# Windowed attention ahead of two expert layers: deeper buffers and another order for the loads of the attention loop

## The chip, the cores and the metric

The program runs on one core of one Trainium2 chip. The metric is the device time of one launch in microseconds: the median of several runs, lower is better. A profile is one further execution, which the hardware profiler recorded.

## The reference, cut to what matters

Three layers follow each other: attention over short windows, then two mixture-of-experts layers. The change touches the first alone.

```python
B, H, S, D = q.shape                      # 4, 8, 768, 64
chunk, left_ctx, right_ctx = (32, 16, 8)
for c in range(S // chunk):
    q_c = q[:, :, c_start:c_end]
    k_full = np.concatenate([mem_k, k[:, :, l_start:r_end]], axis=2)
    v_full = np.concatenate([mem_v, v[:, :, l_start:r_end]], axis=2)
    scores = scale * np.matmul(q_c, k_full.transpose(0, 1, 3, 2))
    a = np.exp(scores - np.max(scores, axis=-1, keepdims=True))
    a = a / (np.sum(a, axis=-1, keepdims=True) + 1e-09)
    out[:, :, c_start:c_end] = np.matmul(a, v_full)
...
x = attention output as 3072 tokens x 512
x = _moe_ref(x)     # 8 experts, a skip score and a top-1 choice for each token
x = _moe2_ref(x)    # 8 experts, all of them for all tokens, weighted
```

## The kernel before

**The attention loop.** The 3072 tokens are cut into 24 tiles of 128 tokens (`NT`), and the loop `for t in range(NT)` near line 500 is a software pipeline. Step t computes the scores of tile t (`qk`, line 279, on PE), their row maxima (`smax`, DVE) and exponentials (`sexp`, ACT). In the same step PE transposes the exponentials of tile t-1 (`a_trans`), multiplies them with the values (`av`, line 317), and DVE scales the result and starts its store (`x_norm`, lines 323 and 324). Tile t-2 is transposed (`x_trans`), tile t-3 goes through the router's small matmul (`gate1`, `fold`). Every fourth step a group of four tiles gets its routing tables, a chain of small DVE and POOL operations spread over the five steps that follow (`step`); PE's share of it are the rank matmuls (`rank`) in steps 9, 13, 17 and 21 and the table matmuls (`table`) two steps later.

**Loads and stores of a tile.** A tile needs queries (`qs`), windowed keys (`kb`) and windowed values (`vw`). The function `load(i)` starts these three transfers, all but one of them on SyncE's queue (SP in the views), which takes its instructions strictly in program order: an issue that has to wait holds up all issues behind it. `qs` and `kb` have three buffers each and `vw` four. The finished tile goes from `x_nat` (three buffers) to the tensor `x_t` in DRAM. DMA issues on SP count on eight semaphores in turn, so an issue also waits until the transfer eight issues earlier has landed.

**Weights fetched beside the loop.** The first expert layer needs its weights in two parts, a rounded copy and a rest. `fetch()` brings one raw chunk of 512 KB into one of three buffers `wraw` (line 188). `conv` makes the two parts: a copy on ACT (line 192) at once, and two subtractions on DVE (line 196) and the next `fetch()`, which are put on the list `defer` and run in the next step. Steps 4, 7, 11, 15 and 19 convert a chunk (`convs`); three more are converted after the loop (`held`). In the order of a step, the store of tile t-1 comes first, then a fetch if there is one, then the loads of tile t+2:

```python
while defer:
    defer.pop(0)()
if t in (1, 2, 3):
    fetch()
if t + 2 < NT:
    load(t + 2)
if t in convs:
    conv(*first[convs.index(t)], defer)
```

**After the loop** comes the rest of the pipeline for the last tiles, the last routing group of eight tiles, and a gather of the tokens of the first expert (`xe_load`), with which the expert layers begin. PE does matmuls there with little else.

Of the kernel before, what the change touches and what calls it, by code (L numbers as in the profile page):

```python
# [8 lines left out]
F32 = mybir.dt.float32  # L9
# [12 lines left out]
NT = N // 128  # L22
TPB = S // 128
# [3 lines left out]
KWIN = NM + 152 + NM  # L27
KEYS = 96
# [22 lines left out]
def kernel(ctx, tc, qT, kT, v, wg, m1_w1, m1_w2, m2_w1, m2_w2, out):  # L51
    nc = tc.nc
# [3 lines left out]
    def pool(name, **kw):  # L56
        return tc.tile_pool(name=name, bufs=1, reuse_waits="tile", **kw)
# [11 lines left out]
    att = att_s.enter_context(pool("att"))  # L69
# [9 lines left out]
    def bank(name, tag, bufs=1):  # L79
        return psum.tile([128, 512], F32, name=name, tag=tag, bufs=bufs)  # L80


    qs = [att.tile([128, 4, 128], F32, name=f"qs{i}") for i in range(3)]
    kb = [att.tile([128, 4, KWIN], F32, name=f"kb{i}") for i in range(3)]
    vw = [att.tile([KEYS, 2, D], F32, name=f"vw{i}") for i in range(4)]

    def load(i, q=nc.sync):
        b, ib = divmod(i, TPB)
        q.dma_start(out=qs[i % 3], in_=qT[:, b, ib])
        nc.sync.dma_start(out=kb[i % 3], in_=kT[:, b, ib])  # L90
        nc.sync.dma_start(out=vw[i % 4], in_=v[b, ib])


# [1 line left out]
    chunk_bf = att.tile([128, 128], BF16, name="chunk_bf")  # L95
    one = att.tile([128, 1], F32, name="one")

    load(0, nc.scalar)
    nc.gpsimd.memset(chunk_bf, 0.0)
    nc.vector.memset(one, 0.0)  # L100
    nc.scalar.activation(out=one, in_=one, func=ACTF.Exp)
# [1 line left out]
    def fill_mask(i):  # L103
        m = masks[i]
        nc.vector.memset(m, 0.0)
        for j in range(2):
            w = NM * (1 - j)
            nc.vector.memset(m[64 * j:64 * j + 1, :, w + 56:w + WIN], NEG)
            nc.vector.memset(m[64 * j + 32:64 * j + 33, :, w:w + 32], NEG)
        if i == 1:  # L110
            nc.vector.memset(m[0:1, :, NM:NM + 16], NEG)
        if i == 2:
            nc.vector.memset(m[96:97, :, 80:WIN], NEG)
# [4 lines left out]
    fill_mask(0)  # L118
    ident = const.tile([128, 128], F32, name="ident")
    make_identity(nc, ident)  # L120
    load(1)
    ones_bf = keep.tile([128, 128], BF16, name="ones_bf")
    nc.gpsimd.memset(ones_bf, 1.0)
    tri_bf = keep.tile([128, 128], BF16, name="tri_bf")
# [117 lines left out]
    sc = {}  # L242
# [8 lines left out]
    def gate1(i, p=None):  # L251
        p = bank("lp_ps", "A", 3) if p is None else p
        t = xT.pop(i)
        for k in range(KD):
            nc.tensor.matmul(p[32 * k:32 * k + 32, 384:512], wg_sb[:, k], t[:, k], start=True, stop=True, tile_position=(0, 32 * k), skip_group_check=True)
        lp[i] = p

    def lp_evac(i):
        s = att.tile([128, 128], F32, name="lp", tag="lp", bufs=2)
        nc.scalar.copy(out=s, in_=lp[i][:, 384:512])  # L260
        lp[i] = s

    def qk(i):
        ib = i % TPB
        mv = {0: 1, TPB - 1: 2}.get(ib, 0)
        sc[i] = []
        for p in range(2):
            s = bank("s_ps", "A", 3)
            if p == 0 and i >= 3:
                gate1(i - 3, s)  # L270
            s = s[:, 0:4 * KEYS].rearrange("p (h k) -> p h k", k=KEYS)
            nc.tensor.matmul(s, chunk_bf, masks[mv], start=True, stop=False, skip_group_check=True)
            sc[i].append(s)
        for hp in range(4):
            for p in range(2):
                d = slice(64 * p, 64 * p + 64)
                for j in range(2):
                    t = slice(64 * j, 64 * j + 64)
                    nc.tensor.matmul(sc[i][p][t, hp], qs[i % 3][d, hp, t], kb[i % 3][d, hp, 72 * j:72 * j + KEYS], start=False, stop=(hp == 3), tile_position=(64 * p, 64 * j), skip_group_check=True)

    def smax(i, p):
        if p == 0:
            mn[i] = [att.tile([128, 2, 4], F32, name=k, tag=k, bufs=2) for k in ("mx", "nm")]
        mx, nm = mn[i]
        nc.vector.tensor_reduce(out=mx[:, p], in_=sc[i][p], axis=AX.X, op=ALU.max)
        nc.vector.tensor_scalar(out=nm[:, p], in0=mx[:, p], scalar1=-scale, scalar2=None, op0=ALU.mult)

    def sexp(i, p):
        if p == 0:
            ex[i] = att.tile([128, 2, 4, KEYS], F32, name="a", tag="a", bufs=2), att.tile([128, 4, 2], F32, name="sm", tag="sm", bufs=2)  # L290
        a, sm = ex[i]
        for hp in range(4):
            nc.scalar.activation(out=a[:, p, hp], in_=sc[i][p][:, hp], func=ACTF.Exp, bias=mn[i][1][:, p, hp:hp + 1], scale=scale, accum_out=sm[:, hp, p:p + 1])

    def a_trans(i, p, eng):
        if p == 0:
            at[i] = att.tile([KEYS, 2, 4, 128], F32, name="at", tag="at", bufs=2)
        q = bank("at_ps", "B", 2)
        for hp in range(4):
            nc.tensor.transpose(q[0:KEYS, 128 * hp:128 * hp + 128], ex[i][0][:, p, hp], ident)  # L300
        eng(out=at[i][:, p], in_=q[0:KEYS])

    def snorm(i):
        sm = ex.pop(i)[1]
        rs = att.tile([128, 4, 2], F32, name="rs", tag="rs", bufs=2)
        nc.vector.tensor_scalar(out=rs, in0=sm, scalar1=1e-9, scalar2=None, op0=ALU.add)
        nc.vector.reciprocal(out=rs, in_=rs)
        ex[i] = rs

    def av(i):  # L310
        p = bank("x_ps", "C", 1)
        t = at.pop(i)
        for pp in range(2):
            for hp in range(4):
                f = slice(128 * hp + 64 * pp, 128 * hp + 64 * pp + 64)
                for j in range(2):
                    nc.tensor.matmul(p[64 * j:64 * j + 64, f], t[:, pp, hp, 64 * j:64 * j + 64], vw[i % 4][:, j, f], start=True, stop=True, tile_position=(0, 64 * j), skip_group_check=True)
        xps[i] = p

    def x_norm(i):  # L320
        x_nat[i] = att.tile([128, D], F32, name="x_nat", tag="x_nat", bufs=3)
        r = ex.pop(i).rearrange("p h q -> p (h q)").unsqueeze(2).to_broadcast([128, H, HD])
        nc.vector.tensor_tensor(out=x_nat[i].rearrange("p (h d) -> p h d", h=H), in0=xps.pop(i).rearrange("p (h d) -> p h d", h=H), in1=r, op=ALU.mult)
        nc.sync.dma_start(out=x_t[128 * i:128 * i + 128, :], in_=x_nat[i])

    def x_trans(i):
        p = bank("xt_ps", "D", 1)
        for k in range(KD):
            nc.tensor.transpose(p[:, 128 * k:128 * k + 128], x_nat[i][:, 128 * k:128 * k + 128], ident)
        xT[i] = p  # L330

    def xt_evac(i):
        t = att.tile([128, KD, 128], F32, name="xT", tag="xT", bufs=2)
        nc.scalar.copy(out=t, in_=xT[i])
        xT[i] = t
# [4 lines left out]
    i = 0  # L340
# [143 lines left out]
    def step(t, slot):  # L484
        for f in steps.pop((t, slot), ()):
            f()

    def fold(i, t=None):
        fold1(i)
        gi, j = where[i]  # L490
        if j == GROUPS[gi] - 1:
            r = Route(gi)
            if t is None:
                return r
            for d, slot, f in ((0, "act", r.logits), (1, "dve", r.choose), (1, "pool", lambda: r.shift(nc.gpsimd)), (2, "act", r.exp), (2, "dve", r.count), (3, "pe", r.rank),
                               (3, "dve", r.gate), (3, "pool", lambda: r.parts(nc.gpsimd)), (3, "dve", r.places), (4, "dve", r.firsts), (4, "dve", r.slots), (5, "pe", r.table), (5, "dve", r.take)):
                steps.setdefault((t + d, slot), []).append(f)

    vcopy, scopy = nc.vector.tensor_copy, nc.scalar.copy
    for t in range(NT):  # L500
        qk(t)
        smax(t, 0)
        if t >= 3:
            lp_evac(t - 3)
        sexp(t, 0)
        if t >= 1:
            a_trans(t - 1, 0, vcopy)
            a_trans(t - 1, 1, vcopy)
        smax(t, 1)
        if t >= 2:  # L510
            x_trans(t - 2)
            xt_evac(t - 2)
        sexp(t, 1)
        if t >= 3:
            fold(t - 3, t)
        step(t, "pe")
        if t >= 1:
            snorm(t - 1)
            av(t - 1)
            x_norm(t - 1)  # L520
        step(t, "act")
        step(t, "dve")
        step(t, "pool")
        while defer:
            defer.pop(0)()
        if t == 0:
            fill_mask(2)
        if t in (1, 2, 3):
            fetch()
        if t + 2 < NT:  # L530
            load(t + 2)
        if t in convs:
            conv(*first[convs.index(t)], defer)
    while defer:
# [20 lines left out]
    q = fold(L)  # L555
# [16 lines left out]
    p = fbank[:, 384:384 + E]  # L572
# [674 lines left out]
    for h, k in ((0, 0), (1, 1), (1, 0), (0, 1)):  # L1247
        f = slice(256 * k, 256 * k + 256)
# [161 lines left out]
    for n in range(1, NU2 + 1):  # L1410
        e, s, half = where_is(n)
        b = n // 2
# [15 lines left out]
        for c in TURN:  # L1428
            if c == "y":
                i = yq.pop(0)  # L1430
# [19 lines left out]
            elif not last:  # L1450
                i = int(c[1])
# [82 lines left out]
```

## Time and profile before

| what | value |
|---|---|
| median of 3 runs | 2334.0 us (2333.48 to 2337.08) |
| the profiled execution's own time | 2338.85 us |
| span of its profile | 2336.1 us |
| PE busy | 2285.4 us, 98% of the span |
| DVE, ACT, POOL busy | 1451.8, 1209.0, 375.0 us |
| mean granted TensorE clock | 0.991 of full speed |

The profiled execution is one run; its time is 2.75 us longer than its span and 4.85 us longer than the median. The shares are averages over stages that differ: the page's row of forty slices shows PE at 7, 7, 8 and 9 tenths in the first four slices and at 9 in all others, and its row of the granted clock shows 8, 8, 9, 9 and then 9. So what PE leaves idle lies at the beginning, in the attention stage, and the stage has to be read by itself.

### The profile page before, as it was taken

The numbers are of one execution on the slowest core, as the hardware profiler recorded it, in microseconds if no ns is written. First come the engines' busy times: TensorE is split into PE (matmuls) and PEld (weight loads), VectorE is DVE, ScalarE is ACT, GpSimd is POOL, SyncE is SP. The second block draws the span as 40 slices with busy tenths as digits, with TensorE's granted clock in tenths as the row PEclk, the third lists the DMA queues.
The fourth block names the chain that finished last, engine by engine and source line by source line (L and its number), as shares of the span: only waits on it lengthen the run. The fifth ranks groups of instructions, "written<-read, shape, count | busy, mean of one in ns | idle before, by whom it ended". The sixth has DMA issues, their size and how long they took to land.

```text
span 2336.1 us, 49229 instructions
## 1 busy us (share of the span) xinstructions
PE 2285.4 (98%) x20016; PEld 2237.9 (96%) x20016; DVE 1451.8 (62%) x2534; ACT 1209.0 (52%) x2508; POOL 375.0 (16%) x393
## 2 busy tenths in 40 slices
PE   7789999999999999999999999999999999999999
PEld 5668988999999999999999999999999999999999
DVE  5766666667765557556755585558555755566555
ACT  5554554554554456445644474446444644455444
POOL 0003424211101111111111102110211021102001
PEclk8899999999999999999999999999999999999999
DMA  7757875775747567776878687877877687867343
GB/s 224 215 164 220 280 260 197 263 231 167 246 175 242 168 212 243 191 212 164 282 176 228 164 258 190 221 190 225 212 207 213 209 230 181 233 181 214 93 132 86
DMA packets 177591, 478.78 MB, mean 205 GB/s; under 512 B 24688, under 2 KB 41584, under 8 KB 177362
## 3 DMA queue, kind: packets, MB, share of 16 engines
q1 hardware_dynamic: 133570, 381.97, 46.9%
q0 software_dynamic: 43232, 92.72, 22.0%
q8 instruction: 158, 2.59, 0.5%
q10 hardware_dynamic: 560, 0.92, 0.1%
q14 instruction: 71, 0.58, 0.1%
HBM read 343.93 MB, written 118.65 MB: 198 GB/s over the span
## 4 chain that ended last, share of the span: by engine, by line
PE 89%; issue 1%; DMA 1%; DVE 1%; ACT 0%; POOL 0%; POOLq 0%; SPq 0%; ACTq 0%; DVEq 0%
PE h_ps L976 14%; PE h_ps L975 14%; PE h_ps L977 14%; PE y_ps L1053 13%; PE y_ps L1054 13%; PE y_ps L1055 13%; PE y_ps L761 1%; PE y_ps L763 1%; PE y_ps L762 1%; PE h_ps L744 1%; PE h_ps L745 1%; PE h_ps L743 1%; DMA wtt<-in_m_w_dram 1%; PE x_ps L898 0%; DVE wl L198 0%
## 5 line engine op out<-in xcount | busy, mean ns | idle before, releaser
L976 PE MATMUL h_ps<-xs,wh 128*128 128x256 f32 x2688 | 760.3, 283 | 0.1
L975 PE MATMUL h_ps<-xs,wh 128*128 128x256 f32 x2688 | 758.3, 282 | 0.3 <-ACT r L942 0.2
L977 PE MATMUL h_ps<-xs,wl 128*128 128x256 f32 x2688 | 756.7, 282 | 0.0
L1053 PE MATMUL y_ps<-wh,cb 128*128 128x256 f32 x2304 | 649.3, 282 | 0.0
L1054 PE MATMUL y_ps<-wl,cb 128*128 128x256 f32 x2304 | 647.2, 281 | 0.0
L1055 PE MATMUL y_ps<-wh,cb 128*128 128x256 f32 x2304 | 645.9, 280 | 0.0
L977 PEld LDWEIGHTS h_ps<-xs,wl 128*128 128x128 f32 x2688 | 507.7, 189 | 0.0
L975 PEld LDWEIGHTS h_ps<-xs,wh 128*128 128x128 f32 x2688 | 506.3, 188 | 0.9 <-ACT r L942 0.7
L976 PEld LDWEIGHTS h_ps<-xs,wh 128*128 128x128 f32 x2688 | 504.9, 188 | 0.6 <-DVE xs L887 0.6
L941 DVE TENSOR_TENSOR cb<-r,cb 128x512 fp32r<-128x512 f32 x384 | 264.7, 690 | 325.0 <-ACT cb L951 324.8
L1053 PEld LDWEIGHTS y_ps<-wh,cb 128*128 128x128 f32 x2304 | 435.2, 189 | 0.1
L1055 PEld LDWEIGHTS y_ps<-wh,cb 128*128 128x128 f32 x2304 | 435.2, 189 | 0.0
L1054 PEld LDWEIGHTS y_ps<-wl,cb 128*128 128x128 f32 x2304 | 433.8, 188 | 0.0
L951 ACT CAST cb<-r 128x512 fp32r<-128x512 f32 x384 | 239.3, 623 | 74.7 <-DVE r L943 74.5
L985 ACT COPY h_ps<-h_ps 128x512 f32<-128x512 f32 x96 | 54.7, 570 | 323.1 <-PE h_ps L977 323.1
L868 DVE TENSOR_TENSOR r<-h_ps,m 128x512 f32<-128x512 f32 x96 | 66.4, 691 | 200.7 <-PE h_ps L977 198.0
L942 ACT ACTIVATE cb<-r 128x512 fp32r<-128x512 f32 x96 | 60.6, 631 | 239.9 <-DVE r L868 239.9
L942 ACT ACTIVATE r<-h_ps 128x512 f32<-128x512 f32 x191 | 114.1, 597 | 119.4 <-PE h_ps L977 115.8
L198 DVE TENSOR_TENSOR wl<-wraw,wh 128x512 fp32r<-128x512 f32 (+2 forms) x148 | 123.4, 854 | 52.3 <-ACT wh L192 51.4
L1093 POOL DMA_DIRECT2D out_dram<-oA x35 | 42.3, 1209 | 630.4 <-ACT wh L192 249.3
L192 ACT CAST wh<-wraw 128x1024 fp32r<-128x1024 f32 (+2 forms) x156 | 113.6, 753 | 48.5 <-DMA wraw<-in_m_w_dram 23.2
L941 DVE TENSOR_TENSOR r<-r,r 128x512 f32<-128x512 f32 x192 | 131.8, 687 | 3.3
(242 smaller groups left out, 3535.5 us busy)
## 6 DMA issues: line engine op xcount, KB each, us to landing
xs<-xd SPq DMA_DIRECT2D x294, 512.0 KB, 7.4
wraw<-in_m_w_dram SPq DMA_DIRECT2D x124, 512.0 KB, 4.9
wtt<-in_m_w_dram SPq DMA_DIRECT2D x112, 256.0 KB, 6.8
xd<-xs SPq DMA_DIRECT2D x42, 512.0 KB, 8.0
wtt<-in_m_w_dram POOLq DMA_DIRECT2D x56, 384.0 KB, 6.1
td<-wtt SPq DMA_DIRECT2D x42, 512.0 KB, 4.5
wtt<-td SPq DMA_DIRECT2D x42, 512.0 KB, 3.8
out_dram<-oA POOLq DMA_DIRECT2D x41, 512.0 KB, 8.8
```

The source lines that it names most:

```text
L192: nc.scalar.copy(out=hi, in_=src)
L198: eng.tensor_tensor(out=lo, in0=src, in1=hi.bitcast(F32), op=ALU.subtract)
L868: add = lambda o, a, b: nc.vector.tensor_tensor(out=o, in0=a, in1=b, op=ALU.add)
L941: tt = lambda o, a, b, op: nc.vector.tensor_tensor(out=o, in0=a, in1=b, op=op)
L942: relu = lambda o, i: nc.scalar.activation(out=o, in_=i, func=ACTF.Relu)
L951: (relu if pos else lambda o, i: nc.scalar.copy(out=o, in_=i))(cb[n, i][:, 0], src)
L975: nc.tensor.matmul(o, wh[:, SLOT[i], k], x[:, 0, k], start=(new and f == 0 and k == 0), stop=False, skip_group_check=True)
L976: nc.tensor.matmul(o, wh[:, SLOT[i], k], x[:, 1, k], start=False, stop=False, skip_group_check=True)
L977: nc.tensor.matmul(o, wl[:, SLOT[i], k], x[:, 0, k], start=False, stop=(k == 1), skip_group_check=True)
L1053: nc.tensor.matmul(o, t[:, 0, c], wh, start=(i != 1 and half == f == j == 0), stop=False, skip_group_check=True)
L1054: nc.tensor.matmul(o, t[:, 0, c], wl, start=False, stop=False, skip_group_check=True)
L1055: nc.tensor.matmul(o, t[:, 1, c], wh, start=False, stop=(half == f == 1), skip_group_check=True)
```

## The change

`load` is split. `load_qk(i)` starts the transfers of queries and keys, which now have four buffers each, and `load_v(i)` that of the values. In step t, `load_qk(t + 3)` is the first thing in program order, and so stands on SP's queue ahead of that step's store of tile t-1; `load_v(t + 3)` comes after the store, where `load(t + 2)` was. Ahead of the loop three tiles are loaded and not two. The raw weight chunks, of which the first three were fetched in steps 1, 2 and 3, are fetched later: one in step 2, those that follow a conversion as before, and two in step 21.

```diff
--- before.py
+++ after.py
@@ -80,14 +80,17 @@
         return psum.tile([128, 512], F32, name=name, tag=tag, bufs=bufs)
 
 
-    qs = [att.tile([128, 4, 128], F32, name=f"qs{i}") for i in range(3)]
-    kb = [att.tile([128, 4, KWIN], F32, name=f"kb{i}") for i in range(3)]
+    qs = [att.tile([128, 4, 128], F32, name=f"qs{i}") for i in range(4)]
+    kb = [att.tile([128, 4, KWIN], F32, name=f"kb{i}") for i in range(4)]
     vw = [att.tile([KEYS, 2, D], F32, name=f"vw{i}") for i in range(4)]
 
-    def load(i, q=nc.sync):
+    def load_qk(i, q=nc.sync):
         b, ib = divmod(i, TPB)
-        q.dma_start(out=qs[i % 3], in_=qT[:, b, ib])
-        nc.sync.dma_start(out=kb[i % 3], in_=kT[:, b, ib])
+        q.dma_start(out=qs[i % 4], in_=qT[:, b, ib])
+        nc.sync.dma_start(out=kb[i % 4], in_=kT[:, b, ib])
+
+    def load_v(i):
+        b, ib = divmod(i, TPB)
         nc.sync.dma_start(out=vw[i % 4], in_=v[b, ib])
 
 
@@ -95,7 +98,9 @@
     chunk_bf = att.tile([128, 128], BF16, name="chunk_bf")
     one = att.tile([128, 1], F32, name="one")
 
-    load(0, nc.scalar)
+    load_qk(0, nc.scalar)
+    load_qk(1)
+    load_v(0)
     nc.gpsimd.memset(chunk_bf, 0.0)
     nc.vector.memset(one, 0.0)
     nc.scalar.activation(out=one, in_=one, func=ACTF.Exp)
@@ -118,7 +123,9 @@
     fill_mask(0)
     ident = const.tile([128, 128], F32, name="ident")
     make_identity(nc, ident)
-    load(1)
+    load_qk(2)
+    load_v(1)
+    load_v(2)
     ones_bf = keep.tile([128, 128], BF16, name="ones_bf")
     nc.gpsimd.memset(ones_bf, 1.0)
     tri_bf = keep.tile([128, 128], BF16, name="tri_bf")
@@ -276,7 +283,7 @@
                 d = slice(64 * p, 64 * p + 64)
                 for j in range(2):
                     t = slice(64 * j, 64 * j + 64)
-                    nc.tensor.matmul(sc[i][p][t, hp], qs[i % 3][d, hp, t], kb[i % 3][d, hp, 72 * j:72 * j + KEYS], start=False, stop=(hp == 3), tile_position=(64 * p, 64 * j), skip_group_check=True)
+                    nc.tensor.matmul(sc[i][p][t, hp], qs[i % 4][d, hp, t], kb[i % 4][d, hp, 72 * j:72 * j + KEYS], start=False, stop=(hp == 3), tile_position=(64 * p, 64 * j), skip_group_check=True)
 
     def smax(i, p):
         if p == 0:
@@ -498,6 +505,8 @@
 
     vcopy, scopy = nc.vector.tensor_copy, nc.scalar.copy
     for t in range(NT):
+        if t + 3 < NT:
+            load_qk(t + 3)
         qk(t)
         smax(t, 0)
         if t >= 3:
@@ -525,10 +534,10 @@
             defer.pop(0)()
         if t == 0:
             fill_mask(2)
-        if t in (1, 2, 3):
+        if t + 3 < NT:
+            load_v(t + 3)
+        for _ in range({2: 1, 21: 2}.get(t, 0)):
             fetch()
-        if t + 2 < NT:
-            load(t + 2)
         if t in convs:
             conv(*first[convs.index(t)], defer)
     while defer:
```

No instruction of PE, DVE, ACT or POOL changes its place in the attention loop; what moves stands on SP. The two further buffers also shift the addresses of later tiles, by which the first copies of the expert stage wait for other earlier users of their memory than before.

On SP, step 5 of the kernel before begins with the store of tile 4, then a weight chunk, and then the three loads of tile 7; the numbers behind `qs`, `kb` and `vw` tell buffers apart:

```order
L324 DMA x_t<-x_nat 128x512
L188 DMA wraw<-in_m_w_dram 128x1024
L89 DMA qs_83<-in_qT_dram 128x512
L90 DMA kb_86<-in_kT_dram 128x672
L91 DMA vw_91<-in_v_dram 96x1024
L324 DMA x_t<-x_nat 128x512
```

The same place after the change, from the beginning of step 5 to the store of step 6:

```order
L89 DMA qs_82<-in_qT_dram 128x512
L90 DMA kb_86<-in_kT_dram 128x672
L331 DMA x_t<-x_nat 128x512
L195 DMA wraw<-in_m_w_dram 128x1024
L94 DMA vw_90<-in_v_dram 96x1024
L89 DMA qs_83<-in_qT_dram 128x512
L90 DMA kb_87<-in_kT_dram 128x672
L331 DMA x_t<-x_nat 128x512
```

The first two rows load queries and keys of tile 8, and the two ahead of the last row those of tile 9: a tile's queries and keys moved from behind the store of step t-2 to the front of step t-3.

On SP at the end of the loop, steps 20 to 23 of the kernel before (the last row is that of three stores):

```order
L188 DMA wraw<-in_m_w_dram 128x1024
L89 DMA qs_83<-in_qT_dram 128x512
L90 DMA kb_86<-in_kT_dram 128x672
L91 DMA vw_90<-in_v_dram 96x1024
L324 DMA x_t<-x_nat 128x512
L89 DMA qs_84<-in_qT_dram 128x512
L90 DMA kb_87<-in_kT_dram 128x672
L91 DMA vw_91<-in_v_dram 96x1024
L324 DMA x_t<-x_nat 128x512 x3
```

The same steps after the change:

```order
L89 DMA qs_85<-in_qT_dram 128x512
L90 DMA kb_89<-in_kT_dram 128x672
L331 DMA x_t<-x_nat 128x512
L195 DMA wraw<-in_m_w_dram 128x1024
L94 DMA vw_93<-in_v_dram 96x1024
L331 DMA x_t<-x_nat 128x512
L195 DMA wraw<-in_m_w_dram 128x1024 x2
L331 DMA x_t<-x_nat 128x512 x3
```

The last tile's queries and keys moved up by a step, and two weight chunks came down to the place that they left.

## Rows read from the trace of the kernel before

**Rows 1.** Stretches of the program: length, busy time (instructions) by engine, clock, DMA.

```profile
core 0: us, PE busy (x) PEld busy (x) DVE busy (x) ACT busy (x) POOL busy (x), PEclk, DMA share, GB/s
2.80:155.75 152.95, 117.10 (x1998) 95.67 (x1999) 99.02 (x297) 83.24 (x420) 8.26 (x39) 0.88 0.72 222
155.75:173.74 17.99, 16.20 (x274) 14.14 (x271) 12.46 (x50) 9.80 (x34) 1.61 (x3) 1.00 0.15 47
...
400.00:2336.00 1936.00, 1929.92 (x16177) 1928.59 (x16176) 1196.04 (x2000) 999.67 (x1884) 277.81 (x254) 1.00 0.70 202
```

**Rows 2.** Waits of PE from 0 to 160 us: total, times, longest.

```profile
PE s_ps L279 <- DMA kb<-in_kT_dram: 31.4, 13, 5.0
PE s_ps L272 <- POOL pad_f L130: 2.8, 1, 2.8
...
```

**Rows 3.** Order in time of SyncE's DMA issues, 38 to 50 us: start, length.

```profile
40.49 0.33 SPq L324 DMA_DIRECT2D x_t<-x_nat  x1
41.73 0.55 SPq L188 DMA_DIRECT2D wraw<-in_m_w_dram  x1
42.37 0.39 SPq L89 DMA_DIRECT2D qs<-in_qT_dram  x1
42.81 0.42 SPq L90 DMA_DIRECT2D kb<-in_kT_dram  x1
43.32 0.38 SPq L91 DMA_DIRECT2D vw<-in_v_dram  x1
...
```

**Rows 4.** Order in time of PE: start, length, what; idle before in brackets.

```profile
12.65 1.81 PE L317 MATMUL x_ps<-vw,at 96*64 96x64 f32 x32
...
40.44 0.89 PE L279 MATMUL s_ps<-kb,qs 64*64 64x96 f32 x32
...
49.65 1.56 PE L279 MATMUL s_ps<-kb,qs 64*64 64x96 f32 x32 [4.43 <-DMA kb<-in_kT_dram]
```

**Rows 5.** Line 90, the loads of `kb`: issue to landing.

```profile
...
DMA to landing us min/median/max: 3.9/5.8/7.9
```

**Rows 6.** SyncE's waits, 14 to 155 us: total, times, longest.

```profile
...
SPq L188 <- DVE wl L196: 5.7, 5, 1.3
...
```

**Rows 7.** Stretches, one loop step each (columns of rows 1): steps 11, 14, 17; sums.

```profile
77.38:81.88 4.50, 4.50 (x101) 3.73 (x97) 4.31 (x15) 3.23 (x18) 0.00 (x0) 1.00 0.64 160
...
92.96:103.41 10.45, 7.13 (x93) 6.17 (x89) 4.51 (x15) 4.56 (x25) 1.33 (x6) 0.67 0.68 221
...
114.06:119.20 5.14, 4.91 (x98) 3.79 (x94) 4.91 (x14) 3.52 (x20) 0.00 (x0) 1.00 0.53 157
...
sum 78.37, PE 61.60 PEld 50.88 DVE 55.39 ACT 45.09 POOL 4.72; mean PE 5.13 PEld 4.24 DVE 4.62 ACT 3.76 POOL 0.39
```

**Rows 8.** The same view, steps 2 to 10: the sum alone.

```profile
...
sum 62.98, PE 47.19 PEld 38.81 DVE 36.93 ACT 33.87 POOL 1.58; mean PE 5.24 PEld 4.31 DVE 4.10 ACT 3.76 POOL 0.18
```

**Rows 9.** Two stretches in which the DMA engines were full (columns of rows 1).

```profile
20.50:26.50 6.00, 5.14 (x86) 4.68 (x86) 3.05 (x9) 2.60 (x13) 0.00 (x0) 0.72 0.98 343
...
66.00:73.00 7.00, 2.04 (x42) 1.49 (x42) 1.46 (x7) 1.20 (x8) 1.33 (x6) 0.70 0.98 285
```

**Rows 10.** DMA issues from 0 to 160 us: count, size, median us to landing.

```profile
vw<-in_v_dram SPq DMA_DIRECT2D x24, 384.0 KB, 6.3
kb<-in_kT_dram SPq DMA_DIRECT2D x24, 336.0 KB, 5.8
qs<-in_qT_dram SPq DMA_DIRECT2D x23, 256.0 KB, 4.2
x_t<-x_nat SPq DMA_DIRECT2D x22, 256.0 KB, 3.0
wraw<-in_m_w_dram SPq DMA_DIRECT2D x8, 512.0 KB, 3.8
```

**Rows 11.** Line 324, the stores of `x_nat`: issue to landing.

```profile
...
DMA to landing us min/median/max: 2.0/2.4/6.2
```

**Rows 12.** Order in time of all engines, 163 to 182 us: ScalarE's late weight copies.

```profile
...
169.75 2.94 ACT L192 CAST wh<-wraw 128x1024 fp32r<-128x1024 f32 x3
...
```

## The prediction

> **What bounds the kernel now.** I read the stretches first. From 400 us to the end PE is busy 1929.92 of 1936.00 us [rows 1]: the expert stage gives nothing back, and whatever makes it start earlier comes off the end. The attention loop, from the first score matmul of step 0 at 2.80 us to that of step 23 at 155.75, takes 152.95 us, of which PE works 117.10 at a mean granted clock of 0.88 [rows 1]. The next view is that of PE's waits: 31.4 us in 13 waits for the landing of `kb`, the longest 5.0 [rows 2]; no other wait of the loop is over 3 us.
>
> Why `kb` is late shows on SP's queue. The store of tile 4 is issued at 40.49, when DVE has finished it at the end of step 5. Behind it a weight chunk waits for a buffer and goes out at 41.73, then `qs` at 42.37 and `kb` of tile 7 at 42.81 [rows 3]. Step 7 wants that `kb` one step later, and PE waits 4.43 us for it, until 49.65 [rows 4]. From issue to landing `kb` takes 3.9 to 7.9 us, median 5.8 [rows 5], while a step without a wait lasts 4.50 [rows 7]: one step of lead is too short. Such a wait is also followed by slow matmuls: the 32 score matmuls take 1.56 us at 49.65 and 0.89 at 40.44 [rows 4], and step 14 shows a granted clock of 0.67 (1.2 GHz in place of 2.4 for two thirds of it) and 7.13 us of PE work, where steps 11 and 17 show 1.00 and 4.50 and 4.91 [rows 7].
>
> **What the change does, part by part.** *Earlier `qs` and `kb`.* They are issued behind the store of step t-1 for step t+3, and so have about two steps more, some 9 us: lead of 13 to 14 us against a longest landing of 7.9 [rows 5]. The waits of 31.4 us go. What is moved past: the stores on SP now stand behind two issues of about 0.4 us each [rows 3], which wait for nothing new, since their fourth buffer was last read one step before. The store itself must land before its `x_nat` buffer is written again three tiles later; it lands in 2.0 to 6.2 us [rows 11], so DVE does not wait. If the queue were so full that a store took over 13 us, DVE's `x_nat` would be late, and PE's transposes and the next store behind it.
>
> *`vw` one step earlier.* It was not waited for; nothing.
>
> *The fetches.* A chunk no longer waits for a buffer (5.7 us in all, on SP alone [rows 6]) ahead of `qs` and `kb`. The first conversions now get chunks that were issued two steps before, about 9 us ahead of a landing with a median of 3.8 [rows 10]. The two chunks of step 21 have some 20 us until ACT's copies at 169.75 [rows 12]. Both cost nothing. If that cover were gone, a copy would be late by one landing, 4 to 8 us, and the expert stage with it.
>
> *The start.* Ahead of `vw` of tile 0 now stand `qs` and `kb` of tile 1, 592 KB [rows 10], under 2 us at 340 GB/s [rows 9]; its first reader starts at 12.65 [rows 4], with `vw` there well before. Nothing again. The same holds for the two waits that new addresses put at the expert stage's first copies: they are for attention work that ended before.
>
> *What is next in the way.* With `kb` in time a step is as long as the busier of PE and DVE. I take steps 2 to 22, which last 62.98 + 78.37 = 141.35 us now [rows 7, 8]; steps 0 and 1, the other 11.6, fill the pipeline and stay. PE at full clock needs 4.50 in a plain step and 4.91 in one with rank matmuls [rows 7]. DVE is at its densest in step 17, 4.91 busy of 5.14 us, or 95.5% [rows 7]; I take that as its ceiling.
> - Steps 2 to 10 (one with rank matmuls): PE 9 x 4.50 + 0.41 = 40.9; DVE 36.93 / 0.955 = 38.7 [rows 8]. PE binds, 40.9.
> - Steps 11 to 22 (three with rank matmuls): PE 12 x 4.50 + 3 x 0.41 = 55.2; DVE 55.39 / 0.955 = 58.0 [rows 7]. DVE binds, 58.0.
>
> Together 98.9. Two engines so evenly loaded, each waiting for the other within a step, lose something at the hand-offs, and DVE's load is uneven. No row shows the loop without waits, so I bound that loss: at least 0, at most 11.1, with which the steps would keep the 141.35 - 31.4 = 110.0 us that they have beside the waits. The steps without a wait lie near the low end (step 11 is PE's work and nothing else [rows 7]), so I take 3. The new sum is 102, and 141.35 - 102 = 39 us are gained: 31 from the waits, 8 from matmuls that no longer run at half clock, less what DVE then holds up.
>
> *A rule against this sum.* PE's work in these 21 steps is 47.19 + 61.60 = 108.8 us against 96.1 at full clock, so the rows put 12.7 us on the clock [rows 7, 8]. The Trainium skill, TensorE: Matmul & The Clock Gate, section on HAM oscillation, charges a throttled stretch with half its length: a mean of 0.88 over 152.95 us would be 36.7 us throttled and an estimated 18.4 lost, and the time 2334 - 31.4 - 18.4 = 2284 us. In these stretches PE was in part waiting, so the rows' smaller figure is the one to use, and here DVE takes a part of it.
>
> *DMA.* Four steps move 4 x (384 + 336 + 256 + 256) KB and one chunk of 512, 5.57 MB [rows 10]. In stretches with the engines full they moved 285 to 343 GB/s [rows 9], so four steps need 16.2 to 19.5 us; the forecast gives them 19.4. It fits, but barely at the low end. A step's burst of 1.26 MB ends before the next store comes, and three tiles of lead even out the steps with a chunk. The last `kb`, that of tile 23, has 31.2 MB issued up to and with it: 91 to 109 us, against 116 when step 23 asks for it. The Trainium skill, DMA: Bandwidth & Descriptors, section "Where 436 GB/s comes from", gives about 358 GB/s for one core's share of HBM, an estimated 15.6 us for four steps; the fullest rows lie just under it, and the sum would not change.
>
> After the loop 17.99 us remain until the gather [rows 1], which no part of the change touches.
>
> **Rivals.**
> - *The waits go, but nothing else* (0.18). DVE's and ACT's work, now hidden in the waits, comes out, and the steps stay at 110.0 us: 2334 - 31.4 = 2303 us. For it speaks that DVE is 95.5% busy in step 17; against it that steps without a wait follow each other at 4.50.
> - *DMA becomes the bound* (0.08). If the engines run dry after each burst until the next store, about 1.1 us (a store's shortest landing, 2.0 us [rows 11], less its transfer, 0.9 at 285 GB/s), and the dry time counts, four steps take 17.7 + 4.4 = 22 us at the middle rate and 24 at the lowest: 116 to 125 us for the 21 steps, 2309 to 2318 us. Against it: a burst is wanted only three steps later.
> - *The change doesn't do what it says* (0.03). If every issue on SP stuck behind the transfer eight issues earlier, the lead would shrink to what it is today, and the time stay at 2334 us. Eight issues are under two steps, so a landing of over 9 us would be needed in general; the longest of `kb` is 7.9 [rows 5].
> - *Slower* (0.02). More transfers in flight could move fewer bytes a second. The last `kb` then decides: it lands after step 23's present start, 155.75 us, if the 31.2 MB come at under 201 GB/s. At 190 it would land at 165 us, and the time would be 2343 us. Against it: even with its idle stretches the loop now moves 222 GB/s [rows 1], and full stretches 285 or more [rows 9].
>
> **How the numbers follow.** The sum is made against the profiled execution, 2338.85 us, which becomes 2299.5; that execution lies 4.85 us above the median, so for the median I forecast 2334.0 - 39 = 2295 us. Its own range is 2287 to 2303 (PE alone as the bound, 21 x 4.50 = 94.5 us, would give 47 us), chance 0.65. With the first rival that makes 0.83, and the range is 2287 to 2307 us. The remaining 0.04 is for a time under 2287, if the fill and the rest after the loop gain as well. Faster by over 0.2% (4.7 us, about what a measurement of this kernel can tell from no change): 0.65 + 0.18 + 0.08 + 0.04 = 0.95. Within 0.2%: 0.03. Slower: 0.02.
>
> **What would show it right or wrong.** PE's waits for `kb` should be under 3 us in all, the granted clock of the loop 0.97 or more, the loop from step 0 to step 23 about 114 us, a step 4.5 to 5.2, DMA busy over 85% in it, and DVE over 85%. `kb` may take longer to land than now and still be early. I would be wrong if PE's waits for `kb` come back in the second half of the loop (DMA is the bound), if the clock is high and steps still last 5.2 (hand-offs), or if ACT waits for `wraw` at a conversion.

## The result, and the profile after

The changed kernel takes 2296.9 us, the median of 4 runs (2295.41 to 2298.76), where the kernel before takes 2334.94 (4 runs, 2333.48 to 2337.08): a ratio of 0.9837 with a 95% interval of 0.982 to 0.9854, 38 us less. The forecast was 2295 us with a range of 2287 to 2307.

The profiled execution after took 2296.07 us. Of its page come first the span and the row of the granted clock. The view behind it is that of stretches, with the columns of [rows 1]: the attention loop to the first score matmul of step 23, what follows until the gather, then steps 2 to 22, steps 2 to 10 of them, and the four steps 11 to 14, which stand for all groups of four.

```profile
span 2294.2 us, 49215 instructions
...
PEclk9999999999999999999999999999999999999999
```

```profile
2.80:114.45 111.65, 105.02 (x1999) 82.84 (x1999) 96.92 (x297) 81.50 (x417) 8.34 (x39) 1.00 0.98 301
114.45:132.47 18.02, 16.22 (x274) 14.13 (x271) 12.50 (x50) 10.19 (x36) 1.61 (x3) 1.00 0.20 69
14.57:114.45 99.88, 96.55 (x1893) 76.74 (x1891) 90.18 (x270) 77.06 (x392) 6.38 (x28) 1.00 0.97 299
...
14.57:56.97 42.40, 40.78 (x797) 32.50 (x795) 35.95 (x99) 32.75 (x167) 1.60 (x7) 1.00 1.00 313
...
56.97:61.51 4.54, 4.54 (x100) 3.76 (x97) 4.35 (x15) 3.51 (x20) 0.00 (x0) 1.00 0.82 216
61.51:66.50 4.99, 4.80 (x93) 3.64 (x89) 4.62 (x17) 4.34 (x20) 0.24 (x1) 1.00 1.03 339
66.50:71.64 5.14, 4.85 (x97) 3.76 (x94) 4.91 (x14) 3.52 (x20) 0.00 (x0) 1.00 0.94 297
71.64:76.14 4.50, 4.40 (x93) 3.60 (x89) 4.21 (x15) 3.40 (x19) 1.35 (x6) 1.00 1.04 279
```

The loop fell from 152.95 us [rows 1] to 111.65, the stretch behind it stayed (17.99, now 18.02), and so did the rest of the span: 2336.1 - 173.74 = 2162.4 us before, 2294.2 - 132.47 = 2161.7 now. All of the gain lies in the loop. PE's work in it fell from 117.10 to 105.02 us with the same matmuls, since the granted clock is 1.00 instead of 0.88. The DMA engines are now busy for 0.98 of it.

PE's waits in steps 2 to 22 (total, times, longest), where [rows 2] had 31.4 us for `kb`:

```profile
PE fbank L359 <- ACT lp L267: 0.9, 4, 0.3
PE x_ps L324 <- issue: 0.4, 1, 0.4
PE s_ps L262 <- issue: 0.2, 1, 0.2
```

No wait for a load is left. How early `kb` is can be read from two orders in time together, SyncE's issues (start, length) and PE's score matmuls of steps 7, 8 and 9:

```profile
25.11 1.52 SPq L89 DMA_DIRECT2D qs<-in_qT_dram  x1
26.68 0.42 SPq L90 DMA_DIRECT2D kb<-in_kT_dram  x1
...
33.67 0.33 SPq L331 DMA_DIRECT2D x_t<-x_nat  x1
34.04 0.43 SPq L195 DMA_DIRECT2D wraw<-in_m_w_dram  x1
34.57 1.68 SPq L94 DMA_DIRECT2D vw<-in_v_dram  x1
36.30 0.43 SPq L89 DMA_DIRECT2D qs<-in_qT_dram  x1
36.77 0.43 SPq L90 DMA_DIRECT2D kb<-in_kT_dram  x1
```

```profile
38.33 0.89 PE L286 MATMUL s_ps<-kb,qs 64*64 64x96 f32 x32
...
42.82 0.89 PE L286 MATMUL s_ps<-kb,qs 64*64 64x96 f32 x32
...
47.67 0.89 PE L286 MATMUL s_ps<-kb,qs 64*64 64x96 f32 x32
```

The `kb` of tile 7 is issued at 26.68 and read at 38.33, 11.65 us later; before, it was issued at 42.81 for a step that could have begun about 4.4 us before 49.65 [rows 3, 4]. The matmuls at 38.33 take 0.89 us, not 1.56 [rows 4]. Some issues last 1.5 or 1.7 us instead of about 0.4.

### The profile page after: what moved, and what is told of

Same layout as the page of the kernel before. It is cut to its first block, busy times and chain, and to the rows that moved or that the text cites. A ratio compares the mean times of both kernels' runs of the same rounds, so it can differ in the third digit from the quotient of the medians.

```text
span 2294.2 us, 49215 instructions
## 1 busy us (share of the span) xinstructions
PE 2271.6 (99%) x20016; PEld 2223.5 (97%) x20016; DVE 1452.0 (63%) x2534; ACT 1206.8 (53%) x2508; POOL 376.0 (16%) x393
## 4 chain that ended last, share of the span: by engine, by line
PE 88%; DVE 3%; DMA 3%; issue 3%; POOL 1%; ACT 1%; SPq 0%; POOLq 0%; ACTq 0%; DVEq 0%
PE h_ps L985 14%; PE h_ps L984 14%; PE h_ps L986 14%; PE y_ps L1062 14%; PE y_ps L1063 14%; PE y_ps L1064 14%; DMA x_t<-x2e,rid 1%; PE h_ps L753 1%; DVE mx L292 1%; PE h_ps L754 1%; PE h_ps L752 1%; DVE at L308 1%; POOL wtt L215 1%; DMA wtt<-in_m_w_dram 1%; PE y_ps L770 0%
## 5 line engine op out<-in xcount | busy, mean ns | idle before, releaser
L877 DVE TENSOR_TENSOR r<-h_ps,m 128x512 f32<-128x512 f32 x96 | 66.4, 692 | 200.5 <-PE h_ps L986 198.1
```

The source lines that it names most:

```text
L877: add = lambda o, a, b: nc.vector.tensor_tensor(out=o, in0=a, in1=b, op=ALU.add)
```

## The experiments

The theory was that of the prediction: `kb` was issued one step ahead behind the step's chunk, PE stood, and the clock fell with it; with the loads in time the steps become as long as PE and DVE make them. The rivals were that one part of the change alone (the chunks, the order, the fourth buffer) carries the gain, that the clock's share is something else, and that DMA sets the pace of the changed loop. "Loop" below is the stretch that [rows 1] calls the attention loop, and it is always that of one profiled execution. The time is a median, and each experiment has runs of the kernel before beside it; the change by itself took 38.0 us off.

**The chunks alone.** The kernel before, with the fetches where the change has them, and no load earlier:

```diff
-        if t in (1, 2, 3):
-            fetch()
         if t + 2 < NT:
             load(t + 2)
+        for _ in range({2: 1, 21: 2}.get(t, 0)):
+            fetch()
```

> The kernel before with one part of the change: one chunk is fetched in step 2, two in step 21, each behind the loads of its step; the lead of queries and keys stays as it was. Theory (the lead counts): only the waits of tiles 3 to 5 shrink, some 3 to 5 us with their slow matmuls; the waits of tiles 7, 10, 14, 18 and 22 stay, since the fetch that follows a conversion still stands in front of the loads. Time 2329 to 2333 us. Rival (the weight chunks are what makes the keys late): over 12 us faster, 2322 us or less.

Measured: 2323.31 us against 2337.13, ratio 0.9949 (0.9934 to 0.9964). PE's waits and the loop:

```profile
PE s_ps L279 <- DMA kb<-in_kT_dram: 25.5, 17, 3.9
```

```profile
2.80:140.09 137.29, 108.11 (x1998) 87.32 (x1998) 98.38 (x297) 82.04 (x417) 8.26 (x39) 0.95 0.80 241
```

The time fell between the two expectations: 13.8 us, more than the theory allowed and less than the rival asked. The waits fell by only 5.9 us (31.4 to 25.5). The loop, though, fell by 15.7, for there are now 17 waits in place of 13, shorter in the mean (1.5 us, 2.4 before), and behind most of them PE's clock stayed up (0.95 for 0.88 over the loop, PE's work 117.10 to 108.11 us). With two chunks fewer in circulation a conversion's next fetch found a free buffer at once: the 5.7 us that line 188 waited on SP [rows 6] are gone from the waits of this trace.

**The loads ahead of the chunk.** The kernel before, where the loads of tile t+2 go in front of the step's deferred subtractions and fetches, still behind the store:

```diff
+        if t + 2 < NT:
+            load(t + 2)
         while defer:
             defer.pop(0)()
...
-        if t + 2 < NT:
-            load(t + 2)
```

> The kernel before with the three loads of a step put ahead of its weight fetch instead of behind it; buffers, lead and fetches stay. So no load stands behind a chunk or behind a chunk's wait for a buffer (5.7 us in five steps), but the lead is still one step. Theory (the chunks in front make the five or six longest waits; the one step of lead makes the others): the waits of tiles 5, 7, 10, 14, 18 and 22 fall to 1 to 2 us and stop taking the clock down, waits 10 to 18 us in all, clock 0.96 or more, loop 120 to 130 us, time 2306 to 2318 us against 2335 of before. Rival (one step of lead is the cause throughout): waits over 22 us in all, time 2320 us or more.

Measured: 2318.9 us against 2335.32, ratio 0.9931 (0.9915 to 0.9948).

```profile
PE s_ps L279 <- DMA kb<-in_kT_dram: 21.2, 15, 2.0
```

```profile
2.80:137.90 135.10, 110.33 (x1999) 89.55 (x1999) 98.66 (x297) 83.07 (x422) 8.27 (x39) 0.94 0.83 251
```

Again between the two. No wait is longer than 2.0 us any more (5.0 in [rows 2]), so the chunk in front made the long ones; 21.2 us of short ones remain, so one step of lead is too short even without it. By itself the order against the chunk brings 16 of the 38 us; the other 22 come only when the loads are issued a step earlier.

**Two tiles ahead with three buffers**, the loads still in front of the store (the changed kernel with `% 3`, without `load_qk(2)` ahead of the loop):

```diff
-        if t + 3 < NT:
-            load_qk(t + 3)
+        if t + 2 < NT:
+            load_qk(t + 2)
```

> The changed kernel with three buffers for queries and keys and loads for step t+2, still ahead of the store. One step of lead more than before, one less than after the change. Theory (one step more is enough, since a key load takes at most 7.9 us in the trace of before and two steps last 9): PE waits under 4 us for keys, time 2295 to 2301 us. Rival (the DMA engines are full, 0.98 of the loop after the change, and only the third tile of lead covers that): waits of 10 us or more come back with half-clock stretches, time 2307 us or more.

**Three tiles ahead, behind the store.** The changed kernel with `load_qk(t + 3)` moved down to `load_v(t + 3)`:

```diff
-        if t + 3 < NT:
-            load_qk(t + 3)
...
         if t + 3 < NT:
+            load_qk(t + 3)
             load_v(t + 3)
```

> The changed kernel with four buffers and loads for step t+3, but queries and keys behind the store, just ahead of the values. Only their place relative to the store is undone. Theory (lead in steps counts, not the place): SP issues them directly behind the store of tile t-1, where after the change those of the following step stood a moment later, so they come a step later for the same tile, two steps ahead of their use. No waits for keys over 3 us, time 2294 to 2300 us. Rival (place counts): waits of over 8 us, 2305 us or more.

Measured: 2298.34 us, ratio 0.9842 (0.9824 to 0.9859), and 2298.65, ratio 0.9839 (0.982 to 0.9857), both against 2337.13. Their loops, first that of the two tiles ahead, then that behind the store:

```profile
2.80:115.97 113.17, 105.33 (x1999) 83.10 (x1999) 97.04 (x297) 82.09 (x421) 8.39 (x39) 1.00 0.96 298
```

```profile
2.80:119.14 116.34, 106.12 (x1999) 83.69 (x1999) 97.58 (x297) 82.61 (x422) 8.39 (x39) 0.99 0.97 291
```

Both came out as the theory had it: the first does not wait for `kb` in steps 2 to 22, the second once, for 0.3 us. Either half of the earlier issue is enough by itself: in front of the store with three buffers, or a tile earlier behind it. Against their own runs of the kernel before they take off 38.8 and 38.5 us, so neither the fourth buffer nor the place in front of the store is worth anything that the medians can tell. The loops are 1.5 and 4.7 us longer than the changed kernel's 111.65, most of it in stops of PE within its matmuls that no load explains (1.7 and 3.5 us in "x_ps <- issue", 0.4 after the change); the last section returns to them.

**The first fetches early again.** The changed kernel with the three early chunks back in steps 1, 2 and 3:

```diff
-        for _ in range({2: 1, 21: 2}.get(t, 0)):
+        for _ in range({1: 1, 2: 1, 3: 1}.get(t, 0)):
```

> The changed kernel with the old fetches: chunks in steps 1, 2 and 3, none in step 21. Theory (the move of the fetches is worth nothing once keys come early): loop length and time within 2 us of the changed kernel, 2295 to 2299 us; buffers are waited for again on SP, some 5 us in all, with no wait of PE. Rival (the early chunks delay keys of tiles 4 to 7 while the DMA engines are full): PE waits 3 to 8 us there, 2300 to 2305 us.

Measured: 2300.02 us against 2337.62, ratio 0.984 (0.982 to 0.9859); loop 116.10 us, no wait for `kb`. So the waits that the rival wanted did not come, and on SP the fetches wait for buffers again, 5.6 us in all, as expected. The loop is 4.5 us longer, which the theory did not allow. PE's waits show where, and PE's order in time shows one such place (idle before in brackets):

```profile
PE x_ps L324 <- issue: 4.1, 4, 1.9
```

```profile
42.12 0.33 PE L324 MATMUL x_ps<-vw,at 96*64 96x64 f32 x2
44.33 1.15 PE L324 MATMUL x_ps<-vw,at 96*64 96x64 f32 x30 [1.89 <-issue]
```

PE stands in the middle of one group of 32 matmuls, behind the second, and nothing that the profile shows releases it. The early chunks need not be the reason: the loop of the experiment just before, with the late fetches, was as long (116.34) and had 3.5 us of the same stops. In time the early chunks cost nothing that can be told: 37.6 us off against 38.0.

**The clock by itself.** The kernel before with all its waits for `kb`, but with idle transposes into an unused part of `fbank` behind the mask matmuls, in the steps that waited, so that PE is busy in most of each wait:

```diff
+FILL = {3: 12, 5: 17, 7: 30, 9: 6, 10: 33, 12: 8, 14: 22, 16: 10, 18: 25, 20: 12, 22: 25}
...
+        for _ in range(FILL.get(i, 0)):
+            nc.tensor.transpose(fbank[:, 384:512], ident, ident)
```

> The kernel before with idle transposes on PE (6 to 33 of them, into an unused piece of a PSUM bank) between the mask matmuls and the score matmuls of the eleven steps with the long waits, about three quarters of each wait. The waits for keys stay, but PE does not stand still in them. Theory (12.7 us of the loop's PE work are due to the lower granted clock after a wait): clock of the loop 0.95 or more, PE's other work about 96 to 100 us in steps 2 to 22, time 8 to 13 us shorter, 2321 to 2327 us. Rival (steps after a wait are long for another reason, such as work of DVE or ACT that piles up): the clock rises and the time stays within 4 us of 2334.

Measured: 2327.75 us against 2337.13, ratio 0.9967 (0.9953 to 0.998). The loop:

```profile
2.80:144.89 142.09, 126.87 (x2199) 104.40 (x2199) 97.41 (x297) 81.61 (x417) 8.33 (x39) 1.00 0.76 239
```

No load moved on SP's queue, PE has 200 transposes more, and the loop is 10.9 us shorter (152.95 - 142.09). The clock stays at 1.00. The waits themselves did not shrink: from the last mask matmul to the first score matmul, steps 2 to 22 take 37.8 us in all before and 39.3 here, read from PE's order in time. So the price of the half clock, taken apart from the waits, is 10.9 us and rather more.

**More and less DMA.** The changed kernel with a second load of each tile's values, from tile 3 on, into spare buffers that nothing reads; and the changed kernel without the loads of the values from tile 4 on:

```diff
         nc.sync.dma_start(out=vw[i % 4], in_=v[b, ib])
+        if i >= 3:
+            nc.sync.dma_start(out=spare[i % 2], in_=v[b, ib])
```

```diff
-        nc.sync.dma_start(out=vw[i % 4], in_=v[b, ib])
+        if i < 4:
+            nc.sync.dma_start(out=vw[i % 4], in_=v[b, ib])
```

> The changed kernel with one more transfer of 384 KB in each step from tile 3 on (values once more, into a spare buffer that nothing reads), 8.3 MB more in the loop, 5.57 to 7.14 MB in four steps. Theory A (after the change the DMA engines, 0.98 busy at 301 GB/s, are as much the bound as DVE and PE): the loop grows by nearly all of the transfer, 8.3 MB at 300 to 320 GB/s, 22 to 28 us, 2319 to 2325 us, and PE waits for keys again. Theory B (the busy share overstates it, and 10 us or more are spare): it grows by under 18 us, 2305 to 2315 us. If the three tiles of lead absorb it: under 5 us.

> The changed kernel without the loads of values from tile 4 on, so that 7.9 MB fewer are moved in the loop; the output uses stale values. Theory (PE does not wait for DMA after the change, DVE and PE set the pace): the loop stays at 111 to 112 us, time within 2 us of 2297. Rival (transfers slow the engines or the pace through the queue): the loop shortens by 3 us or more, to 108 us or less.

Measured with more: 2321.44 us against 2337.62, ratio 0.9931 (0.9911 to 0.995). The loop, and PE's waits:

```profile
2.80:140.00 137.20, 113.47 (x1999) 90.91 (x1999) 98.40 (x297) 82.91 (x422) 8.30 (x39) 0.91 1.04 295
```

```profile
PE x_ps L328 <- issue: 8.4, 5, 2.2
PE s_ps L290 <- DMA kb<-in_kT_dram: 5.2, 3, 2.4
```

One of the three waits for `kb` (about 1.5 us) lies in step 0, where the other kernels wait about as long for the first loads; two are new. With less, the loop alone can be compared, since the stale values change the routing and all that follows (2565.94 us in all):

```profile
2.80:113.57 110.77, 104.38 (x1999) 82.34 (x1999) 96.89 (x297) 81.48 (x417) 8.33 (x39) 1.00 0.73 232
```

The 8.26 MB more (21 x 384 KB) cost 25.55 us of loop, 323 GB/s at the margin, and 21.9 us of time (16.2 us off against 38.0): nearly all of it comes out, as theory A had it. The 7.86 MB less (20 x 384 KB) give only 0.9 us back, though the engines' share falls from 0.98 to 0.73. So DMA does not set the pace of the changed loop, but its work is as long as the loop, and nothing may be added to it.

**DVE's share.** Two edits of the changed kernel that take work off DVE in the steps of 5.14 us: the loop's ten weight subtractions on POOL, and in steps 9, 13, 17 and 21 the second copy of the transposed exponentials (`at`) on ACT.

```diff
+    SUB = [nc.gpsimd]
...
-                defer.append(lambda cols=cols: nc.vector.tensor_tensor(out=lo[:, cols], in0=src[:, cols], in1=hi[:, cols].bitcast(F32), op=ALU.subtract))
+                defer.append(lambda cols=cols: SUB[0].tensor_tensor(out=lo[:, cols], in0=src[:, cols], in1=hi[:, cols].bitcast(F32), op=ALU.subtract))
...
+    SUB[0] = nc.vector
```

```diff
-            a_trans(t - 1, 1, vcopy)
+            a_trans(t - 1, 1, scopy if t in (9, 13, 17, 21) else vcopy)
```

> The changed kernel with the ten subtractions of the five conversions in the loop on POOL instead of DVE, 1.28 us of DVE work in each of steps 5, 8, 12, 16 and 20. Theory (DVE is what makes these steps longer than 4.5 us): steps 8, 12, 16 and 20 fall from 4.8 to 5.0 to about 4.55, the loop from 111.65 to 109 to 110 us, time 2294 to 2296. Rival (PE's own work or hand-offs set these steps): loop over 111 us, time unchanged.

> The changed kernel with the second copy of transposed exponentials (0.68 us on DVE) on ACT in steps 9, 13, 17 and 21, the steps with most DVE work. Theory (DVE sets the length of these steps, 4.9 of 5.14 us): they fall from 5.14 to 4.85 or less, PE's own work there, the loop from 111.65 to 110 to 111 us; the time moves by 1 to 2 us at most, within what can be told. Rival (hand-offs between PE, DVE and ACT set it, or the DMA engines, which are full): the steps stay at 5.1 or others grow by as much.

Measured: 2300.47 us against 2337.62, ratio 0.9844 (0.9826 to 0.9863), loop 115.94; and 2301.29 against 2335.32, ratio 0.9863 (0.9844 to 0.9881), loop 114.07. Neither is better than the change as it is (37.2 and 34.0 us off against 38.0). Of the first, steps 12 and 13, then two equal instructions on DVE and POOL's subtractions beside them:

```profile
63.82:69.42 5.60, 4.80 (x93) 3.64 (x89) 5.24 (x17) 4.39 (x20) 2.75 (x3) 1.00 0.96 275
69.42:73.92 4.50, 4.46 (x98) 3.66 (x94) 3.80 (x12) 3.53 (x20) 0.00 (x0) 1.00 0.68 202
```

```profile
66.24 0.79 DVE L295 TENSOR_SCALAR nm<-mx 128x4 f32<-128x4 f32 x1
...
68.72 0.17 DVE L295 TENSOR_SCALAR nm<-mx 128x4 f32<-128x4 f32 x1
```

```profile
65.73 2.50 POOL L205 TENSOR_TENSOR wl<-wraw,wh 128x512 fp32r<-128x512 f32 x2 [0.73 <-ACT wh L201]
```

It is not step 12, as expected, but step 13 that shrinks, 5.14 to 4.50 us: in its time DVE had run the subtractions, and without them the step is as short as PE's work. Step 12 gives it back, 4.99 to 5.60, since the instruction on `nm` takes 0.62 us longer while POOL subtracts, and what waits for it comes later by as much. The loop as a whole also drew stalls (2.4 us of "issue" on `x_ps`).

Of the second, the stretch of step 13 and PE's waits in the loop:

```profile
66.66:72.39 5.73, 4.82 (x93) 3.77 (x93) 4.50 (x13) 4.12 (x22) 0.00 (x0) 1.00 0.94 300
```

```profile
PE x_ps L324 <- ACT at L308: 2.7, 4, 0.7
```

DVE is busy for 4.50 instead of 4.91 us, and the step is longer, 5.73: PE now waits for the copy on ACT. The theory that the sum of DVE's work sets these steps fell with it. The rival held: PE needs the copy wherever it is made, and on ACT it stands behind that engine's exponentials. Taking the subtractions away shortens these steps and taking the copy away does not. The orders in time show why, first step 13 of the changed kernel, then that with the subtractions on POOL:

```profile
67.30 1.29 DVE L203 TENSOR_TENSOR wl<-wraw,wh 128x512 fp32r<-128x512 f32 x2
68.50 0.55 DVE L292 TENSOR_REDUCE mx<-s_ps 128x4 f32<-128x384 f32 x1
69.14 0.27 ACT L267 COPY lp<-s_ps 128x128 f32<-128x128 f32 x1 [1.62 <-DVE mx L292]
69.46 0.40 PE L359 MATMUL fbank<-fold_f,lp 128*128 128x17 f32 x2 [0.20 <-ACT lp L267]
```

```profile
70.77 0.56 DVE L294 TENSOR_REDUCE mx<-s_ps 128x4 f32<-128x384 f32 x1 [0.47 <-PE s_ps L288]
72.02 0.29 PE L361 MATMUL fbank<-fold_f,lp 128*128 128x17 f32 x2
```

In the changed kernel the row maxima `mx` stand on DVE behind the two subtractions, ACT's next work waits 1.62 us for them, and PE waits for ACT. With the subtractions gone from DVE it is `mx` that waits for PE. In steps 14, 12 and 13 of the changed kernel `mx` starts 0.93, 1.42 and 1.57 us behind the first score matmul, and the steps last 4.50, 4.99 and 5.14 us: what `mx` is late by, the step is longer. With the copy on ACT `mx` starts at 1.57 as before, ACT's part of the chain grows by the copy's 0.58 us, and the step by 0.59. So a chain through three engines sets the length of these steps, in which the order of the work on DVE counts and not its sum; the copy `at` stands behind `mx` on DVE, and taking it off there brings `mx` forward by nothing.

## Why the prediction was right, step by step

| step of the prediction | forecast | measured |
|---|---|---|
| time | 2295 us | 2296.9 us |
| PE's waits for `kb` | under 3 us | none |
| granted clock in the loop | 0.97 or more | 1.00 |
| loop, step 0 to step 23 | about 114 us | 111.65 us |
| steps 2 to 10 (PE binds) | 40.9 us | 42.40 us |
| steps 11 to 22 (DVE binds) | 58.0 us | 99.88 - 42.40 = 57.48 us |
| loss at the hand-offs | 3 us | 99.88 - 98.9 = 1.0 us |
| matmuls at full clock, less what DVE holds up | 8 us | 110.0 - 99.9 = 10.1 us |
| steps 0 and 1 | 11.6 us | 14.57 - 2.80 = 11.77 us |
| behind the loop | 17.99 us | 18.02 us |
| DMA busy, DVE busy | over 85% each | 98%; 96.92 / 111.65 = 87% |
| lead of `kb` | 13 to 14 us | 11.65 and 10.9 us |

**The waits.** The main term, 31.4 us, came in full. The loads ahead of the chunk show that the longest waits were those behind a chunk, as read from [rows 3], and that without a chunk one step of lead still leaves 21.2 us.

**The clock.** The prediction took 8 us for it after DVE's share; it was 10.1. The idle transposes measured the clock alone: 10.9 us in the loop, 9.4 in the time; with the 1.5 us by which the waits grew there, the rows' figure of 12.7 was near. The Trainium skill, TensorE: Matmul & The Clock Gate, section on HAM oscillation, by whose rule 18.4 us were estimated, put too much on it here.

**The hand-offs.** Mis-sized: 3 us were taken out of bounds of 0 and 11.1, and 1.0 was measured over the 98.9. That it came so near is partly luck, since the 98.9 rest on two readings that do not hold. PE's 4.91 in a step with rank matmuls is not what PE needs: with the subtractions on POOL step 13, rank matmuls and all, takes 4.50 us, and PE is busy for 4.46 of them. And DVE's ceiling of 95.5% gave the length of steps 11 to 22 as a whole (57.48 against 58.0), but not for its reason: the plain steps there take 4.49 to 4.54 us, and the excess lies in the two steps behind each conversion (4.99 and 5.14 in steps 12 and 13), which a chain through DVE and ACT sets. Steps 2 to 10, which were to go by PE alone, came out 1.5 us longer than forecast, steps 11 to 22 0.5 shorter. Against PE alone, 94.5 us, the 21 steps lose 5.4.

**DMA.** The sum was right: 33.6 MB (301 GB/s in 111.65 us) fit, barely. One step was wrong in its detail. "A step's burst of 1.26 MB ends before the next store comes" does not hold: the engines are full in steps 12 and 14 and nearly so in 13. And the lead is less than 13 to 14 us, since that was counted from the store: of the 14.0 us between the store at 33.67 and step 9's score matmuls at 47.67, 3.1 are spent on the queue until `kb` goes out at 36.77, 1.3 of them because the issue of `vw` took 1.68 us and the rest on the ordinary issues in between. It cost nothing, since 10.9 us are enough.

**The rivals.** The steps did not stay at 110.0 us (99.9); DMA did not bind, as the loop without the values shows; some issues on SP did stick, but by 1.3 us and not by a step; more transfers in flight moved 301 GB/s over the loop, not under 201.

**From the profile to the median.** The span fell by 41.9 us, the medians by 38. The prediction took the same 39 us off both, though it knew that the profiled execution of before lay 4.85 us above the median; that of after lies 0.8 below its own. So in the profiled execution the loop gained 2.3 us more than forecast (41.3), and in the medians the gain was 1 us less. That the forecast of 2295 missed by only 1.9 us is in part luck: the sum was too small for the execution from which it was read, and that execution was slower than the median. Runs of the kernel before alone reach from 2331.1 to 2341.41 us, so what lies within a few us stays untold.

## What to carry to other kernels

When an engine waits for a load, look at what stands ahead of that load on its queue, and count the lead in steps without the wait: here one step of 4.5 us against a landing of 5.8, with a weight chunk in front in the worst steps, was the fault, and one step more, by either of two ways, removed it. A wait on PE can also cost the slow matmuls behind it, here some 11 us beside 31.4 of waits. Where a step is longer than the busiest engine's work, follow the chain between the engines rather than add up one engine's work. Before more is loaded beside a loop that has been freed of its waits, set its bytes against the rate of the full engines: this one had gone from 0.72 to 0.98 of the DMA engines, and 8.26 MB more cost 25.55 us.

## What the runs showed of the hardware

**PE stops inside a group of matmuls in the loops with busy DMA engines.** The rows "x_ps <- issue" name no releaser. They add up to 8.4 us with the doubled values (DMA share of the loop 1.04), to between 0.2 and 4.1 us in the six kernels at 0.94 to 0.98, in no order with the share (0.4 at 0.98 in the changed kernel, 3.5 and 4.1 in two at 0.97), to 0.3 at 0.83, and to nothing at 0.80 and below (without the values, 0.73, as in the kernel before, 0.72). All 28 "issue" stops of over 0.2 us that PE has in these traces from 14 us to the end of the loop end 1.2 to 1.6 us after a 16 KB packet of the instruction queue q8 has ended, as the traces' DMA packets show. The view of DMA by queue for 41 to 43 us with the early chunks, and for 66.4 to 68 us with the doubled values, ahead of a stall that ends at 69.39 (packets, MB, share of the engines):

```profile
q8 instruction: 1, 0.02, 4.4%
```

```profile
q8 instruction: 1, 0.02, 5.1%
```

That PE waits there for its own instructions, which queue behind the data, fits these rows but was only argued; no run here takes the instruction loads away. It would explain most of the 1.5 to 4.7 us by which loops without a late load were longer than that of the changed kernel.

**SP's long issues go with the same packets, and not with full DMA engines.** They occur in the kernel before as well, here while the DMA engines were busy for 0.60 of the time (SP's order in time, then the stretch):

```profile
63.40 1.71 SPq L89 DMA_DIRECT2D qs<-in_qT_dram  x1
```

```profile
63.20:65.20 2.00, 2.00 (x33) 1.97 (x34) 1.97 (x5) 1.41 (x9) 0.00 (x0) 1.00 0.60 131
```

A packet of q8 is under way from 63.28 to 64.74 us. In the changed kernel all 12 issues of over 0.75 us that SP has from 14 us to the end of the loop overlap such a packet, eleven of q8 and one of the instruction queue q14; for the 1.68 us of `vw` at 34.57 it runs from 34.48 to 35.88. What links the two is not shown.

**POOL's work lengthens small work on DVE.** The 128 x 4 instruction on `nm` took 0.79 us beside POOL's subtraction, 0.17 alone. The Trainium skill, SBUF — State Buffer, section "Who interferes with whom", gives the port pair that the two engines share to the one that issues first, for the whole of that instruction, if the other's instruction uses the pair as well, and counts `tensor_scalar` among those that can. The trace agrees: the 0.79 us end at 67.03, and the first of the two subtractions (half of 2.50 us from 65.73) at 66.98.

**The clock does not fall in proportion to the waits.** With 31.4 us in 13 waits of up to 5.0 us PE's mean granted clock over the loop was 0.88; with 25.5 us in 17 waits of up to 3.9 it was 0.95, with 21.2 us in 15 waits of at most 2.0 it was 0.94, and with idle transposes in the waits 1.00.
